# A fifth group found by threshold search in a fused top-k attention and squared-ReLU kernel

## The chip, the cores and the metric

The kernel runs on one core of a Trainium2 chip. The core has five engines with a queue each: TensorE (PE, matrix multiplies and transposes), VectorE (DVE), ScalarE (ACT), GpSimd (POOL) and SyncE (SP, which only starts transfers here). The metric is the device time of one execution in microseconds; a kernel's time is the median of several executions. A second view is the hardware profiler's record of one execution, with every instruction's start and duration.

## The reference

For 8 batches of 8 heads, 576 positions and head size 64, attention keeps in each row only the scores that reach the row's 32nd largest; the result is laid out as 4608 tokens of 512 and goes through a hidden layer of 2048 with the square of the ReLU:

```python
scores = scale * np.matmul(q, k.transpose(0, 1, 3, 2))
kth = np.partition(scores, -top_k, axis=-1)[..., -top_k:-top_k + 1]
mask = scores >= kth
scores = np.where(mask, scores, -1000000000.0)
scores = scores - np.max(scores, axis=-1, keepdims=True)
attn = np.exp(scores)
attn = attn / (np.sum(attn, axis=-1, keepdims=True) + 1e-09)
return np.matmul(attn, v).astype(np.float32)
...
h = x @ w_in
r = np.maximum(h, 0.0)
g = r * r
return (g @ w_out).astype(np.float32)
```

## The kernel before

**Groups.** Two heads (a head pair, `hp` 0 to 3) are worked on together. A group (batch, hp, gi) is 128 query positions of both heads, so 2 × 128 rows of 576 scores; gi 0 to 3 are the full blocks of 128 positions, and gi 4 (`Z`) joins the last 64 positions of two head pairs. Each batch has 18 groups, all eight together 144. `batch_order` gives their order: in batch 6 the two Z groups come first, then gi 0 of all four pairs, then gi 1, 2 and 3, so that (6, 3, 3), pair 3 and block 3, is the last of its batch.

**An ordinary group** (`top_k`): PE computes the scores into PSUM (`score`, recorded at L582), ACT copies them to the tile `s` (L755), and then the 32nd largest of each row is sought. DVE folds the row's quarters by maximum (three operations, L905), POOL gets the smaller halves by integer additions and a subtraction (three operations, L900), and DVE takes eight maxima at a time (L939, L934, L946) and blanks them out (L943) until the 32nd is in `kth`. ACT then makes the mask (L965).

**A group found by threshold search** (`hunt`, then `hunted`): today four, (2, 2, 3), (3, 2, 3), (4, 2, 3) and (5, 2, 3), listed in `HUNT`. Their scores go to the one tile `hs`. ACT squares and sums each row (first pass of `look`, L776), from which POOL sets a first threshold; then four times ACT counts the scores above the threshold by the sum of signs (L776), and POOL corrects the threshold by small operations on two columns (`tiny`, L783). A last pass counts again and leaves the signs in the one tile `hz`; POOL multiplies the scores by the signs (L812), DVE takes the eight largest below the threshold (two operations, L814) and the wanted one among these is picked (L821). For this the last count must lie between 24 and 31. The answer is in `hth`, and ACT makes the mask from it (L830). The number beside a group in `HUNT` says how many places ahead of the group's mask its search is put into the order.

**Common to both.** PE transposes the scores and adds the mask (`flip`, L585 and L582), ACT takes the exponential (L1021), PE multiplies with the values (`fetch`), ACT copies that (L1087), DVE and POOL divide by the sum (L1094, L1096), and a transposing transfer or PE brings it to the tile `xt`.

**Hidden layer** (`feed`): when all groups of a chunk of 256 or 128 tokens are in `xt`, PE multiplies with `win` (L582), ACT applies ReLU (L1140), POOL (L1152) or ACT (L1155) squares, PE multiplies with `wo`, ACT copies to `o` (L1172), and SP stores. Which engine squares is decided on line 1151:

```python
if last or i * SQ[b] % 8 < SQ[b]:
```

with `last` true where the chunk ends in batch 7; the true branch is POOL. The final chunk has a function of its own (`feed_last`).

**What sets the order.** Each operation is entered into a plan with its engine, an assumed duration, a priority (small goes first) and the operations that it needs. `Plan.schedule` plays this through ahead of time and fixes one order of instructions for each engine; on the chip each engine follows its order and waits on semaphores. The priorities come from a due time `tg`, which advances by `PER` = 5.3 with each ordinary group and by `HN` = 0.3 of that with each searched one (line 1273). The transposes and masks on PE are due at (line 1289)

```python
tt = tg + PER + 2 - TA - TL * max(0, 1 - (NGRP - NH - state["n"]) / NL)
```

where `state["n"]` counts the ordinary groups so far and NGRP − NH is their total. So towards the end the softmaxes get a lead over the hidden layer's work, up to `TL`, over the last `NL` groups.

At the end `verdict` gathers flags from all groups on DVE; if one is up, the whole result is computed again by a plain method.

Of the kernel before, what the change touches and what calls it, by code (L numbers as in the profile page):

```python
# [384 lines left out]
def bass_top_k_attn__then__act_relu_squared_kernel(  # L385
# [24 lines left out]
    def sb(name, shape, dt=FP32, n=None):  # L410
        if n is None:
            return nc.alloc_sbuf_tensor(name, shape, dt)
        return [nc.alloc_sbuf_tensor(f"{name}{i}", shape, dt) for i in range(n)]
# [7 lines left out]
    MA = 21.24  # L421
    MT = 18
    ML = 12
    SQ = (4, 4, 5, 5, 5, 5, 5, 4)
    OWN = 2
    SLACK = 0.3
    TA = 7.2
    TW = -0.14
    TL = 15.79
    WARM = 8  # L430
    COLD = .43
    WP = 6.28
    BW = 1
    WSTEP = 1.2
    WLAST = 770
    NL = 30.09
    HINT = 600
    WD = 1.68
    WC = 1.89
# [22 lines left out]
    c16 = sb("c16", [P, 2, NGRP + 8])  # L462
    c24 = sb("c24", [P, 2, NGRP + 8])
    rzall = sb("rzall", [P, NALL])
    HUNT = {(2, 2, 3): 12, (3, 2, 3): 12, (4, 2, 3): 12, (5, 2, 3): 11}
    NH = len(HUNT)
    NSTEP = 4
    GAIN = (.014, .008, .005, .003)
# [120 lines left out]
    def build(full, weights, pl):  # L589
# [531 lines left out]
        def feed(chunk, xt, tm, step):  # L1121
# [7 lines left out]
            for i, g in enumerate(gs):  # L1129
# [20 lines left out]
                pl.op("act", .15 + w_ / 1200, tf + lag + .5, fr, r=[hh], w=[g])  # L1150
                if last or i * SQ[b] % 8 < SQ[b]:
                    pl.op("gp", .12 + w_ / 580, tf + lag + 1, lambda g=g: gp.tensor_tensor(  # L1152
# [108 lines left out]
        for b in range(NB):  # L1261
# [4 lines left out]
            for i, (hp, gi) in enumerate(seq):  # L1266
                if not full and (b, hp, gi) in HUNT:
                    plan_.insert(len(plan_) - HUNT[b, hp, gi], (hp, gi, 1))
                    plan_.append((hp, gi, 2))
                else:  # L1270
                    plan_.append((hp, gi, 0))
            for hp, gi, kind in plan_:
# [14 lines left out]
                if state.get("more"):  # L1287
                    state.pop("more")()
                tt = tg + PER + 2 - TA - TL * max(0, 1 - (NGRP - NH - state["n"]) / NL)
                pt = attend(gi, st, wt, tt, ws_)  # L1290
# [235 lines left out]
```

## Time and profile before

| | |
|---|---|
| median of 3 executions | 775.21 us (775.09 to 775.52) |
| profiled execution, its own time | 774.41 us |
| its span, first to last instruction | 772.6 us |
| granted TensorE clock | 0.998 |
| memory read, written | 36.70 MB, 9.44 MB (60 GB/s over the span) |

The span is shorter than the execution's own time by what lies before the first and after the last instruction. In the views, PEld is PE's loading of weights, which runs beside its multiplies. A window row gives for each engine the busy time and the number of instructions in that stretch of the span, then the granted clock, the busy share of the transfer engines and GB/s. A group row gives line, engine, operation, output and input, their shapes and count, then busy time in all, the mean of one in ns, and the engine's idle time ahead of them; another form of it gives the shortest, median and longest in ns and the first and last start. A wait row says who waited for whom, for how long in total, how often, and the longest. A timeline row gives start and duration, and in brackets an idle time ahead with what ended it.

### The profile page before, as it was taken

What the parts mean: (1) busy time and instruction counts of PE and PEld (TensorE: products, weight loads), DVE (VectorE), ACT (ScalarE), POOL (GpSimd) and SP (SyncE); (2) the same over time, 40 slices, a digit from 0 to 9 for tenths busy, and PEclk for the clock granted to TensorE, in tenths of its full rate; (3) what the DMA queues carried; (4) which work ended last, traced back from release to release, by engine and by line L of the source; (5) the groups of instructions that cost most, each with busy time, mean ns of one, the idle gap of its engine ahead of it and who ended that gap; (6) DMA issues with size and microseconds to landing.
All of it is one profiled execution on the core that took longest, in us unless ns stands there. A gap on an engine that the chain in (4) does not pass through costs nothing.

```text
span 772.6 us, 27813 instructions
## 1 busy us (share of the span) xinstructions
PE 713.3 (92%) x10680; PEld 528.2 (68%) x10680; DVE 751.6 (97%) x3589; ACT 717.9 (93%) x1141; POOL 687.6 (89%) x720
## 2 busy tenths in 40 slices
PE   7888888999989999998999889999899999999999
PEld 3656666666666676666767657686677777767776
DVE  5999999999999999999999999899999999999996
ACT  4799989899899999999999999999999999998884
POOL 4898998889789899989999899899999998989991
PEclk9999999999999999999999999999999999999999
DMA  7657452032400134103340043301332021100101
GB/s 191 182 137 196 132 135 52 23 83 48 114 11 9 51 83 95 32 16 85 70 99 10 18 111 86 69 6 46 93 82 67 11 68 38 34 23 23 36 23 34
DMA packets 145033, 52.63 MB, mean 68 GB/s; under 512 B 137088, under 2 KB 137344, under 8 KB 144896
## 3 DMA queue, kind: packets, MB, share of 16 engines
q1 hardware_dynamic: 144224, 50.66, 26.7%
q8 instruction: 84, 1.38, 0.8%
q14 instruction: 53, 0.43, 0.2%
q10 hardware_dynamic: 672, 0.16, 0.1%
HBM read 36.70 MB, written 9.44 MB: 60 GB/s over the span
## 4 chain that ended last, share of the span: by engine, by line
ACT 58%; PE 31%; DVE 8%; issue 2%; DVEq 0%; ACTq 0%
PE ps L582 26%; ACT w L965 13%; ACT p L1021 12%; ACT s L755 12%; ACT g L1140 7%; PE ps L585 5%; ACT hz L776 4%; ACT g L1155 3%; DVE f L943 2%; DVE f L905 2%; ACT o L1172 2%; DVE c L939 2%; ACT av L1087 2%; ACT qk L711 1%; ACT qk L712 1%
## 5 line engine op out<-in xcount | busy, mean ns | idle before, releaser
L900 POOL TENSOR_TENSOR f<-u,f 128x864 int32<-128x864 int32 x138 | 236.7, 1715 | 7.6
L965 ACT ACTIVATE w<-s,kth 128x576 bf16<-128x576 f32 x278 | 220.2, 829 | 3.5 <-DVE kth L946 3.5
L943 DVE MATCH_REPLACE8 f<-c,f 128x98 f32<-128x98 f32 (+2 forms) x840 | 221.2, 270 | 0.0
L939 DVE MAX8 c<-f 128x8 f32<-128x98 f32 (+2 forms) x840 | 201.5, 272 | 0.0
L582 PE MATMUL ps<-qk 64*128 64x384 f32 (+3 forms) x1280 | 179.5, 427 | 6.9 <-DVE f L905 5.8
L900 POOL TENSOR_TENSOR u<-f,s 128x576 int32<-128x576 int32 x138 | 166.5, 1206 | 16.6 <-DVE f L905 15.9
L1021 ACT ACTIVATE p<-ps 128x1152 bf16<-128x1152 f32 x144 | 169.1, 1174 | 12.5 <-PE ps L582 11.9
L755 ACT COPY s<-ps 128x1152 f32<-128x1152 f32 x140 | 162.0, 1157 | 17.3 <-PE ps L582 16.9
L582 PEld LDWEIGHTS ps<-qk 64*128 64x128 f32 (+1 forms) x1280 | 130.5, 175 | 39.6 <-DVE f L905 11.8
L582 PE MATMUL ps<-wo,g 128*128 128x512 bf16 (+1 forms) x592 | 142.9, 375 | 2.7 <-ACT qk L714 1.2
L582 PE MATMUL ps<-xt,win 128*128 128x256 bf16 (+1 forms) x1280 | 132.5, 252 | 8.5 <-ACT g L1140 3.6
L900 POOL TENSOR_TENSOR u<-s 128x288 int32<-128x288 int32 x138 | 110.2, 799 | 29.8 <-ACT s L755 26.5
L905 DVE TENSOR_TENSOR f<-ps,f 128x288 f32<-128x288 f32 x280 | 123.7, 442 | 0.1
L946 DVE MAX8 kth<-f 128x8 f32<-128x296 f32 x280 | 120.7, 456 | 0.0
L585 PEld LDWEIGHTS ps<-ident,s 64*128 64x128 f32 x2520 | 96.8, 139 | 30.9 <-ACT w L965 15.1
L582 PEld LDWEIGHTS ps<-xt,win 128*128 128x128 bf16 x1280 | 97.2, 98 | 29.3 <-ACT g L1140 6.0
L934 DVE MAX8 f<-f 128x8 f32<-128x288 f32 x280 | 114.7, 447 | 0.0
L585 PE MATMUL ps<-ident,s 64*128 64x64 f32 x2520 | 107.0, 227 | 4.6 <-ACT w L965 4.1
L1152 POOL TENSOR_TENSOR g<-g 128x512 bf16<-128x512 bf16 x86 | 89.4, 1042 | 2.9 <-ACT g L1140 2.6
L582 PEld LDWEIGHTS ps<-wo,g 128*128 128x128 bf16 x592 | 49.6, 98 | 55.2 <-issue 5.7
L1140 ACT ACTIVATE g<-ps 128x512 bf16<-128x512 f32 x140 | 86.2, 641 | 1.0 <-PE ps L582 0.9
L582 PEld LDWEIGHTS ps<-vb,p 128*128 128x128 bf16 (+1 forms) x1600 | 54.0, 100 | 32.7 <-ACT g L1140 10.5
(104 smaller groups left out, 859.1 us busy)
## 6 DMA issues: line engine op xcount, KB each, us to landing
rv<-in_v_dram SPq DMA_DIRECT2D x64, 128.0 KB, 2.4
rk<-in_k_dram SPq DMA_DIRECT2D x63, 128.0 KB, 2.5
rq<-in_q_dram SPq DMA_DIRECT2D x62, 128.0 KB, 2.5
out_dram<-o SPq DMA_DIRECT2D x31, 256.0 KB, 2.2
g<-in_moe_w_in_dram SPq DMA_DIRECT2D x8, 512.0 KB, 4.2
g<-in_moe_w_out_dram SPq DMA_DIRECT2D x8, 512.0 KB, 4.3
out_dram<-o SPq DMA_DIRECT2D x10, 128.0 KB, 2.3
rq<-in_q_dram SPq DMA_DIRECT2D x32, 32.0 KB, 2.5
```

Of the source, the lines that this page charges most:

```text
L582: return pe.matmul(o, l, r, start=start, stop=stop, skip_group_check=True)
L585: return pe.matmul(o, i, ident, is_transpose=True, skip_group_check=True, **kw)
L755: cp = [pl.op("act", 1.1, tg - LEAD + 1, lambda: act.copy(at(st)[:, :, 0:S], two(banks(ss)[:, FIRST_AT:], SECOND, S)), r=[ss], w=[st])]
L900: return pl.op("gp", dur, prio, lambda: gp.tensor_tensor(o().bitcast(I32), x().bitcast(I32), y().bitcast(I32), op), **kw)
L905: return dve(.36, lambda: vec.tensor_tensor(o(), two(banks(ss)[:, FIRST_AT + c:], SECOND, QUART), x(), ALU.max), r=[ss], **kw)
L934: prev[i] = [dve(.065 + HALF / 960, lambda i=i: vec.max(at(f)[:, i, A + 7:A - 1:-1], at(f)[:, i, M + QUART:E]), after=prev[i] + [low], hol ...
L939: lambda i=i, t=t, c0=c0, c1=c1: vec.max(eighth(t, i), at(f)[:, i, c0:c1]),
L943: lambda i=i, t=t, c0=c0, c1=c1: vec.match_replace(at(f)[:, i, c0:c1], eighth(t, i), at(f)[:, i, c0:c1], NEG), hold=[f])]
L946: ks.append(chain(kth, i, prev[i], .065 + (8 + HALF) / 960, lambda i=i: vec.max(eighth(kth, i), at(f)[:, i, A:M + QUART]), hold=[f]))
L965: masks[i:] = [pl.op("act", .77, tw + .8 * i, lambda i=i: act.activation(at(wt)[:, i, :], at(st)[:, i, 0:S], ACTF.Relu, bias=kth[:, i, n:n ...
L1021: return act.activation(at(pt)[:, :, :].rearrange("p c (h q) -> p h c q", h=2), bass.AP(x.tensor, x.offset, [x.ap[0], [APART, 2], [64, 9], ...
L1140: return act.activation(at(g)[:, 0:kf * nt], bank(hh)[:, 0:kf * nt], ACTF.Relu)
```

## The change

`HUNT` gets a fifth entry, for the last group of batch 6, with its search eleven places ahead of its mask. The last entry of `SQ` goes from 4 to 6. The lead of the last softmaxes is spread over 22 groups instead of 30.09, and is 17.5 at most instead of 15.79. Since NH is the length of `HUNT`, there are 139 ordinary groups instead of 140, the small tables of the search get a fifth column, and all due times behind the search move.

```diff
-    SQ = (4, 4, 5, 5, 5, 5, 5, 4)
+    SQ = (4, 4, 5, 5, 5, 5, 5, 6)
...
-    TL = 15.79
+    TL = 17.5
...
-    NL = 30.09
+    NL = 22
...
-    HUNT = {(2, 2, 3): 12, (3, 2, 3): 12, (4, 2, 3): 12, (5, 2, 3): 11}
+    HUNT = {(2, 2, 3): 12, (3, 2, 3): 12, (4, 2, 3): 12, (5, 2, 3): 11, (6, 3, 3): 11}
```

## The prediction

> **What bounds the kernel now.** I read the busy shares of the whole span first, then the same shares stage by stage, then the waits of the engine that is never idle, and last the chain of work at the end.
>
> ```profile
> span 772.6 us, 27813 instructions
> PE 713.3 (92%) x10680; PEld 528.2 (68%) x10680; DVE 751.6 (97%) x3589; ACT 717.9 (93%) x1141; POOL 687.6 (89%) x720
> ```
>
> VectorE (DVE) sets the pace, but ScalarE (ACT) and TensorE (PE) are only 4 to 5 points behind, so the average doesn't decide. The stages do. The first three rows below hold three of today's four threshold searches, the last four are the stages in which the fifth would run and in which its effect must show:
>
> ```profile
> core 0: us, PE busy (x) PEld busy (x) DVE busy (x) ACT busy (x) POOL busy (x), PEclk, DMA share, GB/s
> 210.00:278.00 68.00, 62.40 (x899) 45.96 (x890) 67.14 (x318) 66.93 (x113) 61.82 (x72) 1.00 0.16 38
> 300.00:369.00 69.00, 62.77 (x928) 45.70 (x929) 68.72 (x326) 68.83 (x116) 63.82 (x73) 1.00 0.22 55
> 489.00:560.00 71.00, 66.17 (x985) 49.90 (x983) 67.90 (x322) 71.00 (x124) 64.89 (x75) 1.00 0.24 53
> 560.00:590.00 30.00, 29.62 (x469) 22.02 (x465) 29.92 (x148) 28.74 (x43) 29.32 (x27) 1.00 0.36 83
> 590.00:657.00 67.00, 64.75 (x1019) 50.61 (x1019) 66.88 (x326) 64.07 (x107) 59.56 (x55) 1.00 0.15 40
> 657.00:700.00 43.00, 41.22 (x665) 30.18 (x662) 42.70 (x208) 38.82 (x58) 39.27 (x37) 1.00 0.12 34
> 700.00:758.00 58.00, 56.12 (x919) 42.77 (x920) 57.66 (x284) 49.97 (x76) 55.74 (x52) 1.00 0.08 22
> ```
>
> Three things are to be seen. From 560 to 758 DVE idles 0.12 + 0.12 + 0.30 + 0.34 = 0.9 us of 198: a group less on DVE is time off that stretch if the others can follow. PE idles 0.38 + 2.25 + 1.78 + 1.88 = 6.3 us there, less than anywhere before. And while a search runs, ACT is full, as in 489 to 560 with 71.00 of 71, where DVE lost 3.1 us. The rows of that loss:
>
> ```profile
> DVE f L943 <- POOL f L900: 2.8, 2, 1.9
> ...
> 484.40 1.17 ACT L755 COPY s<-ps 128x1152 f32<-128x1152 f32 x1
> ...
> 489.25 1.12 ACT L755 COPY hs<-ps 128x1152 f32<-128x1152 f32 x1
> ...
> 492.21 1.13 ACT L755 COPY s<-ps 128x1152 f32<-128x1152 f32 x1
> ...
> 493.42 0.79 POOL L900 TENSOR_TENSOR u<-s 128x288 int32<-128x288 int32 x1 [1.84 <-ACT s L755]
> ...
> 498.43 0.09 DVE L943 MATCH_VALUE_LOAD f<-c,f 128x8 f32 x1 [1.93 <-POOL f L900]
> ```
>
> The scores of the searched group (hs) are copied between those of two ordinary groups, whose copies then lie 7.8 us apart. GpSimd (POOL) waits 1.84 us for the later copy, its subtraction for the group before is late, and DVE waits 1.93 us for that. So a search pays DVE back less than it takes off it.
>
> The end: the last group's last maximum ends on DVE at 758.5, and 14 us follow, mostly on PE.
>
> ```profile
> 757.64 0.83 DVE L946 MAX8 kth<-f 128x8 f32<-128x296 f32 x2
> ...
> 736.80 4.61 PE ps L582 x58
> ...
> 764.66 3.72 PE ps L582 x32
> ...
> 768.57 2.68 PE ps L582 x11
> ```
>
> The chain before that is made of PE stretches without a break, such as the 4.61 us one. The last row is the warm-up multiplies behind the result; the tail itself isn't touched by the change.
>
> **The change part by part.** (1) *The group taken from the ordinary path.* Group (6, 3, 3) is the last of batch 6. DVE loses one group of the pace below, POOL the three integer passes of L900; the score product, its copy, the mask, the softmax and the rest stay the same in number.
>
> ```profile
> 742.12 0.44 DVE L905 TENSOR_TENSOR f<-ps,s 128x288 f32<-128x288 f32 x1
> ...
> 747.50 0.44 DVE L905 TENSOR_TENSOR f<-ps,s 128x288 f32<-128x288 f32 x1
> ...
> L900 POOL TENSOR_TENSOR u<-s x138: 788/798/823, 18.0 to 748.4; 128x288 int32<-128x288 int32 x138
> L900 POOL TENSOR_TENSOR u<-f,s x138: 1196/1206/1222, 20.1 to 749.1; 128x576 int32<-128x576 int32 x138
> L900 POOL TENSOR_TENSOR f<-u,f x138: 1702/1714/1738, 21.4 to 751.3; 128x864 int32<-128x864 int32 x138
> ```
>
> DVE: 747.50 − 742.12 = 5.4 us per group, less about 0.1 us for a reciprocal that falls in it: 5.3 us. POOL: 0.80 + 1.21 + 1.71 = 3.7 us.
>
> (2) *The search added.* By the rows of the four searches:
>
> ```profile
> L776 ACT ACTIVATE hz<-hs,hk x32: 777/850/1029, 219.6 to 542.8; 128x583 f32<-128x583 f32 x32
> ...
> L776 ACT ACTIVATE hz<-hs x8: 678/758/814, 210.1 to 496.2; 128x576 f32<-128x576 f32 x8
> ...
> L776 ACT ACTIVATE hz<-hs,htt x8: 797/871/1054, 266.0 to 549.3; 128x583 f32<-128x583 f32 x8
> ...
> 542.44 1.52 ACT hz L776 x4
> ...
> L812 POOL TENSOR_TENSOR hz<-hz,hs 128x1152 f32<-128x1152 f32 x4 | 8.9, 2228 | 0.3 <-ACT hz L776 0.3
> L783 POOL TENSOR_TENSOR hk<-hk,hot 128x2 f32<-128x2 f32 (+1 forms) x44 | 10.7, 243 | 1.3 <-ACT hz L776 0.9
> L783 POOL TENSOR_TENSOR hk<-hk 128x2 f32<-128x2 f32 (+1 forms) x36 | 7.3, 202 | 0.9
> ...
> L783 POOL TENSOR_TENSOR hk<-hot,hk 128x16 f32<-128x16 f32 x4 | 0.9, 216 | 0.0
> L783 POOL TENSOR_TENSOR htt<-hk 128x2 f32<-128x2 f32 x4 | 0.8, 199 | 0.2
> ...
> L814 DVE MAX8 hk<-hz 128x8 f32<-128x576 f32 x8 | 5.7, 746 | 0.4 <-POOL hz L812 0.4
> L821 DVE TENSOR_REDUCE hth<-hk x4: 151/156/163, 277.6 to 556.7; 128x2 f32<-128x16 f32 x4
> ```
>
> ACT: (32 + 8 + 8)/4 = 12 passes per search, each with a read of its sum. Single records overlap; the chain has two passes with their reads in 1.52 us, so a search takes 6 × 1.52 = 9.1 us of ACT. POOL: (8.9 + 10.7 + 7.3 + 0.9 + 0.8)/4 = 7.1 us, net +3.4 us; POOL idles 67.00 − 59.56 = 7.4 us in 590 to 657, which covers it. DVE: 2 × 0.75 + 0.16 = 1.65 us. **Net on DVE: 5.3 − 1.65 = 3.65 us less.**
>
> (3) *When it runs.* It is put eleven places ahead of its mask, 30 of today's ordinary groups from the end: 758 − 30 × 5.3 = 599; the fourth search stood 49 from the end, at 498, and its copy ran at 489.25, 9 us ahead, so this one's copy comes near 590. The fourth's last step (L821) came at 556.7, 67 us behind its copy; so the fifth spans about 590 to 657, where its mask is due. Its single buffers are free by then:
>
> ```profile
> L585 PE MATMUL ps<-ident,hs x72: 216/223/224, 293.8 to 571.9; 64*128 64x64 f32 x72
> ```
>
> The queries and keys of head pair 3 are there for group (3, 0), which stands just ahead of it: no load is moved, and SP's queue keeps its order; due times behind the search come 3.7 us earlier.
>
> (4) *What it costs others.* ACT idles 67.00 − 64.07 = 2.9 us in 590 to 657 and gets 9.1 us more: 6.2 us are put off past 657, where ACT idles 4.2 + 8.0 = 12.2 us to 758. It fits in the sum, not in the place; queued behind ACT's added passes are score copies, for which POOL and then DVE wait, as at 498.43. The trace bounds the price by what DVE idled in windows with a search: 69.00 − 68.72 = 0.3 us at the low end, 3.1 us at the high end. I take the middle, 1.7 us: the stage is fuller on ACT and PE than the cheap one, but has emptier ones behind it than the dear one had.
>
> (5) *Priorities of the last softmaxes* (TL 17.5 for 15.79, NL 22 for 30.09). With r groups to go the lead was 15.79 × (1 − r/30.09) and is 17.5 × (1 − r/22): at r = 22 it falls from 4.2 us to none, at r = 11 from 10.0 to 8.75, for the last it grows by 1.7. So hidden-layer work of batch 6 goes somewhat ahead of softmaxes on PE, and none is added. What this can gain is bounded by PE's idle time after 657, 1.78 + 1.88 = 3.7 us, and it can lose as much; no row tells the sign. I take nothing.
>
> (6) *Six squares of eight on POOL in the last batch.* The choice on line 1151 reads "last or ...", and chunks of batch 7 are last, so the eighth entry of SQ is never used.
>
> ```profile
> L1155 ACT ACTIVATE g<-g x54: 620/677/850, 75.8 to 690.9; 128x512 bf16<-128x512 bf16 x54
> ...
> L1152 POOL TENSOR_TENSOR g<-g x86: 1029/1040/1055, 74.8 to 755.0; 128x512 bf16<-128x512 bf16 x86
> ```
>
> ACT squares nothing after 690.9 already. This part does nothing: 0.
>
> Sum: 3.65 − 1.7 = 1.95, say **1.9 us less**. The profiled execution took 774.41 us, 1.8 more than its span of 772.6, and stands 0.8 below the median of 775.21. Span 770.7; median 775.21 − 1.9 = **773.3 us**. With the ends of (4) this case reaches from 775.21 − 3.35 = 771.9 to 775.21 − 0.55 = 774.7.
>
> **Rivals.** *A, PE holds the end.* The search takes nothing off PE, whose 6.3 us of idle time in 560 to 758 would have to fall to 2.6 for DVE's 3.65 us to come through. For it: the unbroken PE stretches in the chain. Against: it does idle in each of the four stages, so the order leaves it gaps. Then DVE merely idles longer, and the time stays at 775.2.
>
> [...]
>
> *B, all comes through.* DVE loses 0.3 us at most to the search, and the new order saves a little on PE: 3.65 us or somewhat more, 775.21 − 4 = 771.2. For it: DVE's loss at 300 to 369 was no more. Against: PE idled 6.2 us there, and 2.25 in the new place.
>
> *C, slower: ACT overflows in 590 to 657.* ACT's 6.2 us that don't fit are put off; if what waits is hidden-layer relus (L1140), PE loses matmuls in that stretch and has no idle time later to make them up. Then the end moves by 6.2 less DVE's gain, 6.2 − 3.65 = 2.55 us: 777.8. It decides from the point at which PE's new idle time passes 3.65 us. For it: ACT and PE are both fuller there than in any earlier window with a search before the search is counted. Against: 12.2 us of ACT idle time behind it.
>
> *D, the search misses.* If one of the group's 256 rows ended with fewer than 24 or more than 31 scores above its threshold, a flag would start the whole computation again, and the time would be some 775 us longer at the least. Following the search by its constants on the reference's inputs, all 256 rows end between 24 and 31, so this is only kept for rounding.
>
> **How the numbers follow.** My forecast has 0.50, A 0.17, B 0.08, C 0.24, D 0.01. A measurement of this kernel can tell about 0.2%, 1.55 us, from no change. Of my case 0.36 lie below 773.66 and 0.14 within 0.2%. Faster: 0.36 + 0.08 = 0.44; same: 0.14 + 0.17 = 0.31; slower: 0.25. The range runs from B's 771.2 to just past C, 778.0; my own case alone has 771.9 to 774.7.
>
> **What would show it.** DVE: two maxima over 576 elements more, ten ordinary maxima, six replacements and three folds fewer, busy time 3.6 us down. ACT: passes of L776 from 48 to 60, and 99% busy or more near 590 to 657; squares on ACT still 54. If my loss is right, DVE idles 1 to 3 us in 560 to 758 in waits for L900's results or for score copies. If PE idles more than 6.3 us in that stretch with the end later, C was right; if PE idles as much and DVE more, A. A PE stretch that ends with less than 2.6 us idle would be B. I am wrong in the step itself if the span falls by more than 4 us or if the squares move.

## The result, and the profile after

| | before | after |
|---|---|---|
| median, 20 executions each on one chip | 775.08 us (774.34 to 776.56) | 776.86 us (775.80 to 778.91) |
| ratio after to before, 95% interval | | 1.0023 [1.0016, 1.0030] |
| profiled execution, its own time | 774.41 us | 778.91 us |
| its span | 772.6 us | 777.1 us |

The change makes the kernel 0.2% slower; 1.9 us less had been forecast. Of the 20 executions after, 13 lie between 775.80 and 777.14 us and seven between 778.02 and 778.91, and none of the seven has a mean granted TensorE clock of 1.000, while seven of the 13 have. The profiled execution is the slowest of the 20 and holds a stretch at half clock between 590 and 657 us, shown below.

The busy shares of the whole span after:

```profile
span 777.1 us, 27825 instructions
PE 714.8 (92%) x10680; PEld 529.6 (68%) x10680; DVE 748.8 (96%) x3567; ACT 724.5 (93%) x1165; POOL 690.0 (89%) x740
```

DVE lost 2.8 us of work (751.6 before), and ACT got 6.6 us (717.9). So the work moved in the direction that was meant, but the time did not follow. The stages after, in the windows of the prediction and one more for the end:

```profile
core 0: us, PE busy (x) PEld busy (x) DVE busy (x) ACT busy (x) POOL busy (x), PEclk, DMA share, GB/s
560.00:590.00 30.00, 29.38 (x440) 21.95 (x441) 29.85 (x146) 28.89 (x45) 29.32 (x28) 1.00 0.38 87
590.00:657.00 67.00, 61.94 (x909) 46.62 (x907) 63.60 (x306) 65.05 (x117) 57.45 (x65) 0.97 0.13 35
657.00:700.00 43.00, 41.18 (x767) 32.69 (x761) 42.08 (x199) 42.22 (x66) 41.49 (x46) 1.00 0.12 35
700.00:758.00 58.00, 56.58 (x891) 42.64 (x890) 57.63 (x286) 50.59 (x78) 55.82 (x51) 1.00 0.08 23
758.00:777.00 19.00, 17.74 (x252) 13.20 (x249) 10.43 (x43) 9.22 (x19) 4.24 (x5) 1.00 0.14 49
```

From 560 to 758 DVE now idles 0.15 + 3.40 + 0.92 + 0.37 = 4.8 us where it idled 0.8 (the prediction's 0.9 took 0.12 us for the first stage, whose row gives 30.00 − 29.92 = 0.08), and PE 0.62 + 5.06 + 1.82 + 1.42 = 8.9 us where it idled 6.3. ACT is nearly full from 657 to 700 (0.8 us idle, before 4.2). Among DVE's waits from 560 to 758, the longest is the one that the prediction had read off the fourth search; before, it didn't occur there:

```profile
DVE f L943 <- POOL f L900: 2.3, 3, 1.8
```

The second place is behind the last maximum. First the rows before, then after: the last maxima (L946), the divisions of the last two groups (L1094, L1069), the flags' comparisons (L1393 to L1395) and the last copy into `xt` (L1074).

```profile
757.64 0.83 DVE L946 MAX8 kth<-f 128x8 f32<-128x296 f32 x2
...
759.94 0.17 DVE L1094 RECIPROCAL rzall<-av 128x2 f32<-128x2 f32 x1 [0.67 <-ACT av L1087]
760.03 0.43 DVE L1393 TENSOR_TENSOR fcmp<-c 128x280 f32<-128x280 f32 x1
...
761.86 0.17 DVE L1069 RECIPROCAL rzall<-ps 128x2 f32<-128x2 f32 x1 [0.36 <-PE ps L582]
...
762.81 0.23 DVE L1074 COPY xt<-ps 128x128 bf16<-128x128 bf16 x1 [0.45 <-PE ps L585]
```

```profile
760.11 0.83 DVE L946 MAX8 kth<-f 128x8 f32<-128x296 f32 x2
...
764.31 0.17 DVE L1094 RECIPROCAL rzall<-av 128x2 f32<-128x2 f32 x1 [2.55 <-ACT av L1087]
...
765.56 0.45 DVE L1395 TENSOR_TENSOR fcmp<-kth,fcmp 128x278 f32<-128x278 f32 x1
765.93 0.17 DVE L1069 RECIPROCAL rzall<-ps 128x2 f32<-128x2 f32 x1
...
766.83 0.23 DVE L1074 COPY xt<-ps 128x128 bf16<-128x128 bf16 x1 [0.41 <-PE ps L585]
```

The last maximum ends at 760.94 (758.47 before), and 16.2 us follow it instead of 14.1. From that point to the last copy it takes 5.9 us instead of 4.3. The last-but-one group's division waits 2.55 us for ACT's copy, and the flags' comparisons, which filled a wait before, now end where the last division begins. On ACT the rows after say why the copy is late:

```profile
760.04 1.13 ACT L1021 ACTIVATE p<-ps 128x1152 bf16<-128x1152 f32 x1 [0.85 <-PE ps L582]
...
761.97 1.07 ACT L1140 ACTIVATE g<-ps 128x512 bf16<-128x512 f32 x2
762.99 1.13 ACT L1021 ACTIVATE p<-ps 128x1152 bf16<-128x1152 f32 x1
764.01 0.26 ACT L1087 COPY av<-ps 128x130 f32<-128x130 f32 x1
```

Two ReLUs of hidden-layer work and the last exponential now go ahead of it. PE, at the same time, has more left to do:

```profile
764.10 1.03 PE L582 MATMUL ps<-wo,g 128*128 128x512 bf16 x4
...
767.55 0.59 PE L582 MATMUL ps<-wo,g 128*128 128x512 bf16 x2
768.07 1.74 PE L582 MATMUL ps<-xt,win 128*128 128x128 bf16 x28
```

The first of these rows and the one before the last hold the first and the last of 16 wide second products (4 + 6 + 4 + 2) of the last-but-one chunk. Before, they stood ahead of the end of the last maximum: 32 second products were left behind it, now 48.

The half clock, as two windows of the profile after, and one of another execution of the same kernel (776.76 us, granted clock 1.000 over the whole span):

```profile
645.00:648.60 3.60, 1.96 (x17) 1.23 (x15) 3.56 (x14) 3.60 (x10) 2.48 (x4) 1.00 0.00 0
648.60:652.10 3.50, 3.50 (x12) 2.20 (x12) 3.50 (x22) 2.72 (x5) 2.93 (x5) 0.51 0.00 0
```

```profile
644.47:647.88 3.41, 1.57 (x13) 1.01 (x12) 3.36 (x13) 3.41 (x10) 2.28 (x4) 1.00 0.00 0
```

In the profile after, PE is busy only half of the first window, while ACT is full, and the clock halves for the next 3.4 us. The other execution comes to the same work 0.75 us earlier, in its row: PE is half busy there too (one of its product records is missing), and yet the clock stays. Why it stays isn't shown. What the half clock does to one piece of work is seen on the eight score products of that stretch, in the profile after and in the other execution:

```profile
650.09 2.19 PE L582 MATMUL ps<-qk 64*128 64x192 f32 x8
```

```profile
648.66 1.24 PE L582 MATMUL ps<-qk 64*128 64x192 f32 x8
```

### The profile page after: what moved, and what is told of

Its sections match the earlier page's. It is cut to its first block, busy times and chain, and to the rows that moved or that the text cites. A ratio compares the mean times of both kernels' runs of the same rounds, so it can differ in the third digit from the quotient of the medians.

```text
span 777.1 us, 27825 instructions
## 1 busy us (share of the span) xinstructions
PE 714.8 (92%) x10680; PEld 529.6 (68%) x10680; DVE 748.8 (96%) x3567; ACT 724.5 (93%) x1165; POOL 690.0 (89%) x740
## 4 chain that ended last, share of the span: by engine, by line
ACT 62%; PE 28%; DVE 8%; issue 2%; POOL 0%; DVEq 0%; ACTq 0%; POOLq 0%
PE ps L582 24%; ACT w L965 14%; ACT p L1021 13%; ACT s L755 12%; ACT g L1140 7%; ACT hz L776 4%; PE ps L585 4%; ACT g L1155 3%; DVE f L943 2%; DVE f L905 2%; ACT av L1087 2%; ACT qk L711 2%; ACT o L1172 1%; DVE c L939 1%; ACT qk L712 1%
## 5 line engine op out<-in xcount | busy, mean ns | idle before, releaser
L965 ACT ACTIVATE w<-s,kth 128x576 bf16<-128x576 f32 x276 | 217.4, 831 | 3.7 <-DVE kth L946 3.6
L755 ACT COPY s<-ps 128x1152 f32<-128x1152 f32 x139 | 161.2, 1159 | 17.5 <-PE ps L582 17.0
L905 DVE TENSOR_TENSOR f<-ps,f 128x288 f32<-128x288 f32 x278 | 122.9, 442 | 0.2
L946 DVE MAX8 kth<-f 128x8 f32<-128x296 f32 x278 | 120.4, 457 | 0.0
```

Source lines behind the costliest of these rows:

```text
L755: cp = [pl.op("act", 1.1, tg - LEAD + 1, lambda: act.copy(at(st)[:, :, 0:S], two(banks(ss)[:, FIRST_AT:], SECOND, S)), r=[ss], w=[st])]
L905: return dve(.36, lambda: vec.tensor_tensor(o(), two(banks(ss)[:, FIRST_AT + c:], SECOND, QUART), x(), ALU.max), r=[ss], **kw)
L946: ks.append(chain(kth, i, prev[i], .065 + (8 + HALF) / 960, lambda i=i: vec.max(eighth(kth, i), at(f)[:, i, A:M + QUART]), hold=[f]))
L965: masks[i:] = [pl.op("act", .77, tw + .8 * i, lambda i=i: act.activation(at(wt)[:, i, :], at(st)[:, i, 0:S], ACTF.Relu, bias=kth[:, i, n:n ...
```

## The experiments

All ratios are against the kernel before on the same chip, with 95% intervals. "Tail" is the time from the end of the last maximum (L946) to the end of the span, "the stretch" is 560 to 758.

**Each part alone.** The fifth entry of `HUNT` alone:

```diff
-    HUNT = {(2, 2, 3): 12, (3, 2, 3): 12, (4, 2, 3): 12, (5, 2, 3): 11}
+    HUNT = {(2, 2, 3): 12, (3, 2, 3): 12, (4, 2, 3): 12, (5, 2, 3): 11, (6, 3, 3): 11}
```

> The fifth searched group alone, with the old priorities of the last softmaxes (TL 15.79, NL 30.09). Theory S (the search itself costs what it saves: ScalarE is full in its stretch, and VectorE waits there): about as the changed kernel, 1.5 to 2.5 us above before, VectorE idle 2 to 4 us in 590 to 657. Theory P (the new priorities leave hidden-layer work to the end): 1 to 2 us below before, with a tail behind the last maximum of 14 us.

Measured: 780.83 us, 1.0062 [1.0047, 1.0076]; tail 18.8 us. That is slower than either theory had it. The priorities alone:

```diff
-    TL = 15.79
+    TL = 17.5
...
-    NL = 30.09
+    NL = 22
```

> The new priorities alone (TL 17.5, NL 22), with four searched groups. Theory S: within 0.7 us of before. Theory P: 1.5 to 2.5 us above before, the tail behind the last maximum 2 us longer (16 us for 14).

Measured: 777.58 us, 1.0026 [1.0014, 1.0039]; tail 16.3 us, DVE idle 0.8 us in the stretch as before. And the changed kernel with the search's work taken out:

```diff
-            st, hz = tile("hs"), tile("hz")
-            score(gi, qks, tg, st)
-            used = [0]
+            st, skip = tile("hs"), k == NH - 1
+            _, cp = score(gi, qks, tg, st)
+            th = [pl.op("dve", .09, tg + HD, lambda t=t, x=x: vec.memset(t[:, :, k:k + 1], x), after=cp)
+                  for t, x in ((hth, .13), (htt, .14)) if skip]
+            if skip: return st, th
+            used, hz = [0], tile("hz")
```

> The changed kernel without the work of the fifth search: the thresholds of group (6, 3, 3) are set to a constant, so that group's output isn't the reference's; 9 us of ScalarE, 7 us of GpSimd and 1.6 us of VectorE are left out, and the group still isn't sorted on VectorE. Theory S: 4 us or more below the changed kernel, so 2 us or more below before. Theory E (TensorE holds the last 200 us, whatever VectorE saves): within 1 us of before, with TensorE idle in 560 to 758 no more than before, 6.3 us, and VectorE idle 4 us or more.

Measured: 781.15 us, 1.0075 [1.0060, 1.0089]. Less work, and the slowest of the three. Its last maximum ends early, at 757.8, but the tail is 21.5 us; a row of PE near its end:

```profile
769.20 1.91 PE L582 MATMUL ps<-wo,g 128*128 128x512 bf16 x10
```

Second products of the last-but-one chunk (512 wide) run there, in the middle of the last chunk's (256 wide). Every edit that changes a due time gives a new order of the last two batches, and in these three the order alone is worth 2 to 7 us of tail. So the parts don't add: 0.62% and 0.26% alone, 0.23% together. Comparisons that keep the order fixed had to follow.

**In the order of before, one engine lightened or loaded.** DVE less some 3.4 us: in six groups of batch 6 one of the passes over 288 elements runs over 8 (that part of the maxima is left out). In the trace twelve passes then take 0.17 us instead of 0.45.

```diff
-                                at(f)[:, i, A + 7:A - 1:-1], at(f)[:, i, M + QUART:E]),
+                                at(f)[:, i, A + 7:A - 1:-1], at(f)[:, i, (E - 8 if 116 <= n < 122 else M + QUART):E]),
```

> The kernel before, in its own order on every engine, with VectorE's work made 3.5 us shorter: in the last six ordinary groups of batch 6 the second kind of maximum (L934) looks at 8 elements instead of 288, so their thresholds aren't the reference's. It is what the change means to save, without a search and without a new order. Theory D (VectorE holds the end): 3 us or more below before. Theory E (TensorE holds the last 200 us): within 1 us of before. Theory O (the new order is what costs): says nothing of this run, but needs it to be no slower.

PE less some 3.6 us: 16 of 32 second products of two chunks of batch 6 are left out. (Where 16 such products stand in a row, in the last experiment below, they take 3.63 us; the expectation's 3.9 is a little high.)

```diff
-                        for fb in range(2 * sub, 2 * sub + 2):
+                        for fb in range(2 * sub, 2 * sub + (1 if b == NB - 2 and chunk[0][1] < 256 else 2)):
```

> The kernel before, in its own order, with TensorE's work made 3.9 us shorter: in the first two hidden-layer chunks of batch 6, 16 of the 32 second products (512 columns, 0.24 us each) are left out, so those tokens' output isn't the reference's. Theory E: 2 us or more below before. Theory D: within 1 us of before.

Both edits at once:

> Both cuts, in the order of before: thresholds of six groups and the output of two chunks aren't the reference's. If either engine alone hides the other's gain (theories D and E both partly right): 3 us or more below before, and more than the sum of the two alone. Theory E alone: as the TensorE cut.

And ACT more: added ReLU passes into memory that nothing reads, ahead of the ReLUs that the plan starts between 594 and 649. The expectation has 14 passes and 6.7 us; the run's trace shows 12 passes (1153 instructions on ACT instead of 1141), and ACT's busy time is 6.2 us longer.

```diff
-            ins = o.fn()
+            ins = o.fn(extra=594 < o.start < 649) if e == "act" and o.fn.__name__ == "fr" else o.fn()
...
+                    if extra: act.activation(spot(len(spent)), bank(hh)[:, 0:512], ACTF.Relu); spent.append(1)
```

> The kernel before, in its own order, with 14 more ScalarE passes of 0.48 us, 6.7 us in all, each ahead of a ReLU between 594 and 649, into memory that nothing reads. Theory S (ScalarE is full there and everything waits for it): 2 us or more above before, with VectorE idle 2 us or more in 590 to 657. Theories E and D: within 1 us of before, since ScalarE idles 12 us behind that stretch.

| edit in the order of before | median, us | ratio | tail, us |
|---|---|---|---|
| DVE −3.4 us | 776.23 | 1.0006 [0.9996, 1.0016] | 14.1 |
| PE −3.6 us | 775.57 | 1.0000 [0.9991, 1.0010] | 14.0 |
| both | 774.87 | 0.9993 [0.9983, 1.0002] | 14.0 |
| ACT +6.2 us | 781.11 | 1.0068 [1.0055, 1.0081] | 14.1 |

Neither saving alone gains anything that can be measured, both together at most a little; ACT's load comes through by 5.3 of 6.2 us. In the run with less work on DVE, its busy time in the stretch is 2.5 us shorter (194.64 instead of 197.17) and its idle time longer by as much. A part of the stretch, and the wait that took the gain (560 to 757):

```profile
630.00:660.00 30.00, 27.71 (x439) 22.14 (x439) 27.98 (x149) 29.28 (x52) 25.96 (x24) 1.00 0.19 47
```

```profile
DVE f L905 <- ACT s L755: 2.4, 5, 0.7
```

DVE idles 2.0 of these 30 us (before: none), in front of score copies on ACT. With ACT loaded, DVE idles 3.9 of 40 us and the same wait is 4.8 us from 560 to 757:

```profile
590.00:630.00 40.00, 35.96 (x556) 27.07 (x559) 36.06 (x175) 38.09 (x62) 33.81 (x31) 1.00 0.11 32
```

```profile
DVE f L905 <- ACT s L755: 4.8, 5, 1.7
```

**In the order of after, the search's passes made short.** First another execution of the kernel after, unchanged:

> The changed kernel, a second look. In its first profile TensorE's clock was granted at half for 3.4 us from 648.7, behind two waits for ScalarE's copies (1.15 and 0.49 us). If that is what parts its executions near 776 from those near 778.5, an execution near 776 shows no such stretch, and one near 778.5 does.

Measured: 776.76 us, span 774.9, clock 1.000; DVE idles 198.00 − 194.43 = 3.6 us in the stretch, the tail is 16.2 us again.

```profile
560.00:758.00 198.00, 186.10 (x3021) 144.39 (x3044) 194.43 (x942) 187.07 (x303) 184.95 (x188) 1.00 0.16 40
```

Then the fifth search's passes over 8 columns, with a constant as its threshold:

```diff
-                    wider(hz, i, j > 0), wider(st, i, j > 0), func, accum_out=acc(i, i + 1), **kw[i]),
+                    wider(hz, i, j > 0)[:, 0:8 if k == NH - 1 else None], wider(st, i, j > 0)[:, 0:8 if k == NH - 1 else None],
+                    func, accum_out=acc(i, i + 1), **kw[i]),
```

> The changed kernel in its own order on every engine, with the fifth search's 12 ScalarE passes over 8 columns instead of 576 and 583, and its threshold set to a constant, so group (6, 3, 3)'s output isn't the reference's. About 5 us of ScalarE's time are left out. Theory S (ScalarE's passes cost the gain in 590 to 657): 2 us or more below the changed kernel, VectorE idle in 590 to 657 under 2 us instead of 3.4. Theory E (TensorE's fixed work holds the end from 600 on): within 1 us of the changed kernel's executions near 776, the last maximum earlier and the tail behind it longer.

Measured: 2388.04 us. The constant, 0.13, lay above the threshold that the shortened search had reached, the flag went up, and the plain method ran behind. That says nothing of the passes, but it prices the miss of rival D: 1612 us on top of the 776. With the constant at 1e-6 the flag stays down:

> The changed kernel's order, but the fifth search's six pairs of passes run over 8 columns instead of 576 or 583, so about 7 us of its 9 us on ScalarE are gone in 590 to 657; its threshold is put to a constant, so the masked output of this one group is not the reference's. In this order the rest of the work is untouched. If the passes themselves cost the time (ScalarE overflows), the end comes 3 to 6 us earlier than the changed kernel's: 771 to 774 us, and TensorE's idle time in 560 to 758 falls from 8.9 us towards 6. If the new order is at fault and the passes only fill gaps, it stays within 1 us of the changed kernel, 776 to 777 us, and the 16 wide second products stay behind the last maximum.

Measured: 775.03 us, 0.9994 [0.9983, 1.0005], against 1.0023 for the changed kernel: 0.3%, some 2 us, for 4.0 us less on ACT (720.7 us busy over the span instead of 724.7; the expectation's 7 us is too much). That lies between the two expectations: the passes do cost time, but only a part of what they occupy. The stretch with short passes:

```profile
560.00:758.00 198.00, 187.06 (x3041) 145.61 (x3061) 195.40 (x949) 184.68 (x307) 185.99 (x190) 1.00 0.16 41
```

DVE still idles 2.6 us there. PE's idle time can't be compared with that of the profile after, since 70 matmul records are missing here. The tail is 16.1 us, so the second half of the loss was still there.

**The search in another place.** Ten places ahead with the old priorities (`SQ` ends in 6 here too, and is never read there), and in batch 1, where ACT has room:

```diff
+    HUNT = {(2, 2, 3): 12, (3, 2, 3): 12, (4, 2, 3): 12, (5, 2, 3): 11, (6, 3, 3): 10}
```

> The kernel before with a search for group (6, 3, 3) put ten places ahead of its mask instead of eleven, and with the old priorities of the last softmaxes. If the loss comes from ScalarE's passes wherever they stand in batch 6, it is as slow as the fifth search alone at eleven places, 779 to 781 us. If the loss hangs on how the fixed order happens to fall, one place can be worth several us either way: anything from 773 to 781 us.

```diff
+    HUNT = {(1, 2, 3): 12, (2, 2, 3): 12, (3, 2, 3): 12, (4, 2, 3): 12, (5, 2, 3): 11}
```

> The kernel before with its fifth search in batch 1, group (1, 2, 3), twelve places ahead, instead of batch 6; old priorities. There ScalarE idles 17 us and TensorE 20 us of the 180 from 20 to 200, so the passes fit. If VectorE's group is worth its 3.65 us wherever ScalarE and TensorE have room, the marks of the later work (the first search of batch 2) come 2 to 4 us earlier and the end is at 771.5 to 774 us. If the later, balanced stretches set the end regardless of what is gained ahead of them, the time stays at 775 us or above.

The first took 777.30 us, 1.0026 [1.0017, 1.0036], tail 16.2 us. The second took 786.07 us, 1.0133 [1.0111, 1.0154], the worst of all. Its stages show that the added search was paid for elsewhere:

```profile
20.00:200.00 180.00, 152.12 (x2335) 115.97 (x2345) 178.56 (x851) 168.73 (x265) 164.50 (x162) 0.99 0.43 107
200.00:560.00 360.00, 326.24 (x4948) 249.76 (x4980) 347.35 (x1653) 351.89 (x577) 325.02 (x352) 0.99 0.24 57
```

```profile
DVE f L943 <- POOL f L900: 6.8, 11, 2.3
DVE f L905 <- ACT s L755: 5.0, 7, 1.2
```

In 20 to 200, with the added search, DVE idles 1.4 us. Behind it, from 200 to 560, with the same four searches as before, it idles 12.7 us instead of 4.8, in waits for POOL and ACT (the last two rows, 200 to 560; 2.8 and 0.9 us before), and the granted clock is 0.97 in two of the stages there. Neither expectation had this: the order of all later work had moved, and it was a worse one. Two further tries: the search ten places ahead and the last-but-one chunk's second products due earlier (the diff), and a search twelve places ahead with four priorities chosen anew besides (its expectation has the values):

```diff
-                    pl.op("pe", .432, to + lag + step * sub / 2 - (27 if chunk is CHUNKS[-2] else 0), fo,
+                    pl.op("pe", .432, to + lag + step * sub / 2 - (45 if chunk is CHUNKS[-2] else 0), fo,
```

> As the search ten places ahead with the old priorities, but the second products of the last-but-one chunk get a priority 45 ahead of their due time instead of 27, so that they run before the last maximum as in the kernel before. If the tail is that work, the tail falls to about 14 us and the time from 777.3 to about 775.3 us. If these products merely push other work of TensorE back, it stays at 777 us or above.

> The fifth search twelve places ahead of its mask, the last-but-one chunk's second products 38 ahead of their due time, and four priorities chosen anew (MA 21.77, TA 7.09, TL 13.69, NL 27.47). Nothing is left out. If the fifth search can pay once the order of the last two batches suits it, 772 to 774.5 us; if the balance of VectorE, ScalarE and TensorE takes it back in any order, 775 us or more.

Measured: 777.68 us, 1.0025 [1.0016, 1.0034], and 777.91 us, 1.0034 [1.0021, 1.0046], with tails of 16.0 us both. But in both traces the 16 wide products still stand behind the last maximum, only earlier in the tail. So the earlier due times did not do what they were meant to, and an order with a fifth search and these products ahead of the last maximum has not been run. No version with a fifth search beat the kernel before.

**The tail.** In the order of after, 15 of the 16 wide second products are narrowed:

```diff
-                            ins = mm(bank(op_)[0:n_, :], at(gs[fb // kf])[:, c:c + n_], wo[:, fb, :], fb == 0)
+                            w = 64 if chunk is CHUNKS[-2] and fb else 512
+                            ins = mm(bank(op_)[0:n_, 0:w], at(gs[fb // kf])[:, c:c + n_], wo[:, fb, 0:w], fb == 0)
```

> The changed kernel's order, but of the 16 second products of the last-but-one chunk, which stand behind the last maximum there, 15 work on 64 columns instead of 512, so columns 64 to 511 of these 128 tokens are not the reference's; some 2.9 us less TensorE work in the last 15 us. If this work is the longer tail, the tail falls from 16.2 us to about 14 and the time by about 2 us against the changed kernel: near 774.8. If another wait holds the tail (the last division, the squares on GpSimd), the time stays within 0.5 us of 776.8.

Measured: 778.95 us, 1.0037 [1.0024, 1.0050], not faster than with the products (1.0023); the tail is 17.3 us. Two of its windows, and its PE rows at the end:

```profile
763.90:767.30 3.40, 1.56 (x31) 1.14 (x29) 2.75 (x9) 0.38 (x4) 1.15 (x2) 1.00 0.00 0
767.30:770.70 3.40, 3.26 (x30) 3.16 (x31) 1.20 (x4) 2.33 (x6) 0.00 (x0) 0.53 0.20 77
```

```profile
766.30 0.23 PE L585 MATMUL ps<-ident_bf,x 128*128 128x128 bf16 x1 [1.42 <-DVE x L1071]
...
767.44 3.15 PE L582 MATMUL ps<-xt,win 128*128 128x128 bf16 x28 [0.30 <-ACT xt L1102]
```

PE now waits for the softmax (1.42 us for L1071), is busy 1.56 of 3.40 us, and the next 3.4 us run at half clock: the 28 first products take 3.15 us instead of 1.74. All ten executions had a mean clock of 0.998 or less. So this run didn't isolate the products; the short passes were added:

> Both cuts at once in the changed kernel's order: the fifth search's passes over 8 columns with a constant threshold (that group's masked output is not the reference's), and 15 of the 16 second products of the last-but-one chunk on 64 columns (columns 64 to 511 of these tokens are not the reference's). If the passes (about 2 us) and the tail (2 us) are separate prices that add up, the time is 772.5 to 773.3 us, some 2 us below the kernel before: what VectorE's shorter work is then worth. If they hide each other, it is no better than the better of the two alone, 774.8 to 775.

Measured: 774.52 us, 0.9990 [0.9978, 1.0002]. The two prices don't add up: the tail is still 15.7 us. The chain of waits at its end, in order of time, names what holds it when the products are gone:

```profile
757.68 0.97 ACT g L1140 x2
758.65 1.08 ACT p L1021
...
759.92 0.17 DVE rzall L1094
760.09 0.51 DVE fcmp L1394
...
761.18 0.45 DVE fcmp L1396
761.63 0.09 DVE rzall L1069
```

The fcmp rows are the flags' three comparisons (one line further down than in after). They stand between the divisions of the last two groups, and here they are on the chain. Last, they were moved behind the last copy (L1074), once with both cuts, and once with all the work in place and the products due 40 ahead instead of 27:

```diff
-        x = pl.op("dve", .4, 1e6, lambda: vec.tensor_tensor(fc, c16[:, :, 0:G], c24[:, :, 0:G], ALU.min), after=kths, order=rzs[-2:-1])
+        x = pl.op("dve", .4, 1e6, lambda: vec.tensor_tensor(fc, c16[:, :, 0:G], c24[:, :, 0:G], ALU.min), after=kths, order=masked)
```

> As both cuts at once (the fifth search's passes over 8 columns with a constant threshold, and 15 of 16 second products of the last-but-one chunk on 64 columns: that group's masked output and columns 64 to 511 of these tokens are not the reference's), with the three comparisons for the flags behind the last division's copy besides. With the products gone, the chain through the last softmax is alone: if the comparisons lie on it, the tail falls from 15.7 us to about 14.2 and the time from 774.5 to about 773. If they don't, it stays at 774.5.

> The changed kernel with two moves at its end and nothing left out. VectorE's three comparisons for the flags (1.5 us), which stand between the divisions of the last two groups there, come behind the last division's copy; and the last-but-one chunk's 16 second products get a priority 40 ahead of their due time instead of 27, which puts them ahead of the last value products. If the longer tail is these two chains side by side, the tail falls from 16.2 us to 14.5 or 15 and the time by 1 to 1.5 us against the changed kernel, to 775.3 to 775.9. If the late exponential on ScalarE holds the tail alone, it falls by less than 0.5 us.

With the cuts: 773.45 us, 0.9984 [0.9975, 0.9992], tail 14.9 us. The comparisons did lie on the chain, for 0.8 us of the tail. With all the work in place: 780.10 us, 1.0070 [1.0056, 1.0083], tail 20.3 us, against the expectation of 775.3 to 775.9. The rows of that miss, on PE and DVE:

```profile
760.08 3.63 PE L582 MATMUL ps<-wo,g 128*128 128x512 bf16 x16
763.54 0.48 PE L582 MATMUL ps<-vb,p 128*128 128x65 bf16 x10
...
764.53 0.17 DVE L1094 RECIPROCAL rzall<-av 128x2 f32<-128x2 f32 x1 [5.57 <-ACT av L1087]
```

The 16 products now run as one block, still behind the last maximum but ahead of the value product of the last-but-one group. That product starts 5.4 us behind the end of the last maximum instead of 1.9 us, and the division waits 5.57 us. Here, work taken from behind a chain and put in front of it delayed the chain by nearly its full length.

## Why the prediction was wrong

The forecast was 773.3 us with 771.2 to 778.0 as its range; 776.86 us lies in the range, on the wrong side of no change, and the range holds it only because of the slower rival C at 777.8. Two terms of the sum failed: the tail, taken at nothing, cost 2.0 us, and DVE's added idle time, taken at 1.7 us, came to 2.8.

**Steps (1) and (2), the work moved: right in kind, too large in size.** L776 has 60 passes, the squares on ACT stay 54, the fifth search's copy came at 595.3 and its answer at 673.3, 5 and 16 us later than step (3) had them. In the profile shown, DVE's work fell by 2.8 us of 3.65 foreseen, ACT's busy time rose by 6.6 of 9.1 us, POOL's by 2.4 of 3.4 us.

**Step (4), the price on others: mis-sized.** I took 1.7 us of DVE idle time. In the execution at full clock DVE idles 198.00 − 194.43 = 3.6 us in the stretch against 0.8 before, so 2.7 us; 4.0 us in the profile that holds the half clock. The first is inside the bounds of 0.3 to 3.1, at the high end. The bounds had been drawn from searches in places where ACT and PE were less full.

**What bounds the kernel: the reading that failed first.** "A group less on DVE is time off that stretch if the others can follow" was read as likely, because DVE idled 0.9 of 198 us. The run with 3.4 us less on DVE in an unchanged order, 1.0006 [0.9996, 1.0016], shows that the others can't follow: score copies on ACT then hold it. An engine busy 99.6% of a stage isn't alone in holding it when two others are at 92 to 97%. Rival A (PE holds the end) was too simple as well: 3.6 us less on PE alone also gains nothing.

**"The tail itself isn't touched by the change": wrong.** This is the step that turned the sign, and with it step (5), where I took nothing: the priorities alone lengthened the tail by 2.1 us. With the whole change the tail went from 14.1 to 16.2 us. The account can be closed between two executions that run at full clock from the sixth ordinary fold (L905) on (granted 1.00 from 24.54 to 772 us before, 1.000 over the whole span of the other execution of after). The rows are the sixth fold before, whose last maximum is shown above, and the sixth fold and the last maximum in the other execution of after:

```profile
33.83 0.44 DVE L905 TENSOR_TENSOR f<-ps,s 128x288 f32<-128x288 f32 x1
```

```profile
34.41 0.44 DVE L905 TENSOR_TENSOR f<-ps,s 128x288 f32<-128x288 f32 x1
...
757.96 0.83 DVE L946 MAX8 kth<-f 128x8 f32<-128x296 f32 x2
```

The fold starts 0.58 us later and the last maximum ends 0.32 us later, at 758.79 instead of 758.47, so 0.3 us were gained up to there, of the 1.9 forecast. In that time DVE worked 3.1 us less and idled 2.8 us more. The tail took 2.0 us. Together that is 1.7 us more, where the medians of 20 show 776.86 − 775.08 = 1.8. So of the distance to the forecast some 2 us lie in the tail, 1.1 us in DVE's added idle time and the rest in the smaller saving. The diff names no line of the tail, but the due times behind the search and the lead move every later operation, and what stands behind the last maximum is set by them. The runs show two chains of nearly equal length in it: PE with 16 wide products more, and the last softmax with two ReLUs, a late copy and the flags' comparisons in line. Cutting the first leaves the second: the runs with both cuts shorten the tail to 15.7 and, with the comparisons moved, to 14.9 us. No execution with the products alone cut ran at full clock, so their own price isn't shown.

**Rival C: its mark came, if by little, and its account holds only in part.** PE idled 8.9 us, over its 6.3, with the end later, but in the profile that holds the half clock. The other execution shows 11.9 us with 70 PE records missing, all of them second products; 23 of these lie in the stretch, and such products start 0.22 us apart in the traces, so an estimate is 11.9 − 23 × 0.22 = 6.8 us. ACT's load does cost time: 5.3 us for 6.2 us in the order of before, and about 2 us for 4.0 us in the order of after. It is put off past 657, where ACT idles 0.8 us up to 700 instead of 4.2. But the loss has another part besides, the tail. C had ACT's overflow pushing hidden-layer ReLUs out of 590 to 657; that the wide products turned up behind the last maximum for that reason is only argued, since the priorities alone, with no fifth search, also leave 47 recorded second products there.

**Step (6): right.** The choice on line 1151 never reads the eighth entry of `SQ`, and after the change POOL squares 86 times and ACT 54 times, as before.

**What stays open.** Whether the fifth search can pay at all with an order made for it. Seven orders with a fifth search and the whole work in place were run, the change among them, and all were slower than before. The lowest ratio with a fifth search, 0.9984, leaves out part of the work.

## What to carry to other kernels

Where three engines are above 90% and one order is fixed ahead of time, an engine's work taken off is worth nothing until a run in the same order shows that the time follows; test that first, with the work shortened in place, before moving work to another engine. A change to a due time or a priority changes the whole order behind it: read the stages behind the edit and the tail as parts of the change. And where two chains end within about half a microsecond of each other, as in this tail (16.1 us, and 15.7 us with the products cut), neither shows its price when it is cut alone.

## What the runs showed of the hardware

In the profile after, the granted TensorE clock was at half (0.50) twice, from 27.40 to 30.81 and from 648.63 to 652.04 us, and in the profile before once, from 21.12 to 24.53 us: 3.41 us each time. In the 3.41 us ahead of the drop at 648.63 PE was busy 1.76 us, and in the run with the narrow products 1.56 of the 3.40 us from 763.90, with the clock at 0.53 in the 3.40 us that followed; its longest single waits there were 1.15 and 1.42 us. In the other execution of after PE was busy 1.57 of 3.41 us in the same thin stretch, one product record missing, and the clock stayed. How long PE is busy doesn't tell the cases apart by itself: in the profile after, 3.41 us with 2.11 us busy (from 23.99) were followed by a drop, and 3.41 us with 1.98 us busy (from 64.95) were not. What sets off a drop isn't shown.

The price of one drop can be read from the two executions of after. Ahead of it, PE's transposes of `rk` start 0.75 us apart (647.02 and 646.27), behind it the ten products with `vb` 2.38 us (655.98 and 653.60), and the last maxima 2.15 us (760.11 and 757.96). So the drop took 1.6 us on PE, and 1.4 us of it were there at the last maximum. In the run with the narrow products PE had some 2.9 us less work in the tail (an estimate, 15 products of 0.22 us cut to an eighth), the profiled execution had a drop there, and the kernel stood at 1.0037 instead of 1.0023: taking work off PE saved no time there.
